# Softmax attention and soft mixture of experts: 1 / sum applied to x by GpSimd instead of to the probabilities, x transposed back for the logits, the order planned anew

## The chip, the cores and the metric

The kernel runs on one core of one Trainium2 chip. The metric is the device time of one launch in microseconds (us). The kernel before was timed three times: 593.55, 597.59 and 598.43 us, median 597.59 us.

Engine names are those of the profile: PE is TensorE (PEld its weight loads), DVE is VectorE, ACT is ScalarE, POOL is GpSimd, SP is the queue that issues the DMAs. SBUF is the on-chip memory, PSUM the accumulator memory that PE writes.

## The reference

Inputs are q, k and v of shape (8, 8, 576, 64): batch, heads, tokens, head width. All is float32.

```
scores = q @ k.T / 8                           # 576 x 576 for each head
scores = where(scores >= rowmax - tau, scores, -1e9)
attn   = exp(scores - rowmax);  attn /= (attn.sum(-1) + 1e-9)
x      = attn @ v                              # heads side by side: 4608 tokens x 512
logits = x @ phi                               # phi is 512 x 32 slots
d      = softmax of logits over the 4608 tokens
slot_input = d.T @ x                           # 32 x 512
slot_out = relu(slot_input[e] @ w1[e]) @ w2[e] # 8 experts with 4 slots each, F = 1024
c      = softmax of logits over the 32 slots
out    = c @ slot_out                          # 4608 x 512
```

Since `attn @ v` is linear in each row of attn, the division by the row's sum can be done on the probabilities, before the product with v, or on the rows of x, after it.

## The kernel before, in words

The 64 heads are worked off as 32 pairs (8 batches of 4 pairs), two heads on the two halves of the partitions. The function `pair` makes the work of one pair, `dispatch` the work that follows the fourth pair of a batch. After the last batch comes a tail with the experts and the output, which the change doesn't touch.

One pair has nine score tiles of 128 query rows by 576 keys: two heads times four row blocks of 128, and a ninth with the 64 rows left over of both heads. For each tile:

1. PE makes the scores in PSUM (L504; L509 for the ninth tile).
2. DVE finds the row's negated maximum `nmx`. Tiles 1, 3, 5 and 7 (AWAY) are moved out of PSUM by the same instruction, into the SBUF tile `ss` (L518); the others stay in PSUM (L522).
3. ACT makes exp into the SBUF tile `p` (L531; `pL` for the ninth tile).
4. POOL makes the threshold `thr` from `nmx`, one number for each row (L534).
5. DVE sets the probabilities under the threshold to 0 and sums the row into `r`, in one instruction (L538). It reads `ss` or PSUM, and `p`.
6. After two tiles of one row block, POOL adds 1e-9 to the sums (L545), DVE takes the reciprocal `ri` (L548), and POOL multiplies the probabilities of both tiles by it, 128x576 each (L552). The ninth tile has the same three steps of its own.
7. PE transposes the scaled probabilities into PSUM (L429), and ACT copies them to the SBUF tiles `pTa`, `pTb`, `pTl` (L434).

When the row blocks 0 and 1 (pTa) or 2, 3 and the left-over rows (pTb) are there, PE multiplies by v (L599, two groups of 20 matmul records). This gives x transposed, 128 (two heads of 64) x 576 tokens, which ACT copies to `xT` (L434). PE transposes the first 512 tokens of it back to token rows, and ACT copies them into the batch's tile `x`, 128 x 4 x 512. `dispatch` makes the logits from the four `xT` of the batch (L664), and later the sum `d.T @ x` from `x` (L734).

At the start of each pair POOL also multiplies the loaded keys by 1/8 (L484).

PSUM is split into four regions of two banks each. A score tile, a transposition and a pair of matmul outputs each take a region until its last reader is done. There are two `ss` tiles, four `p` tiles (each for the two heads of one row block), five `xT` and one `x`.

**What sets the order.** All of this is recorded as operations by `Order.add`, with an engine, a duration and a nominal time. `Order.plan` then goes through them with a model of the engines: an operation can start when its operands are there (LAT and SAME are the delays that it assumes after an operation) and a buffer is free; of those that can, each engine takes the one with the lowest nominal time. `TABLE` holds a correction of the nominal time for each operation: of the first, a middle and the last pair, of even, odd and last batches, and of the softmax at the end. The order that comes out is fixed: each engine works through its list strictly in that order, and an instruction that waits holds up all behind it on its engine.

## Time and profile before

| What | Value |
|---|---|
| Times of the three runs | 593.55, 597.59, 598.43 us; median 597.59 us |
| The profiled execution, first to last instruction | 595.4 us |
| Mean granted TensorE clock | 0.978 |
| Busy share of the span: PE, DVE, ACT, POOL | 92%, 83%, 75%, 69% |
| First two pairs (start of the span to the ninth tile of the second pair) | 38.0 us |
| One middle pair without dispatch | 14.67 us |
| Four middle pairs with one dispatch | 62.5 us |
| From the last pair's last copy to x to the end | 72 us |

The page gives no time of the profiled execution beside its span. The median of the three runs is 2.2 us above that span, and the span lies among the three.

A row of a group reads: line, engine, operation, output <- inputs, partitions x elements, count | busy time in us, mean ns of one | idle time of the engine just before them and what ended it. A row of the waits reads: who waited <- for whom: us in total, times, longest. A row of the chain reads: start us, duration us, what; "issue" is time in which an engine waited for nothing that the profile shows. A row of a source line reads: count: duration ns min/median/max, first and last start. A row of the stretches gives the busy us of each engine in a stretch of the span, the granted clock, the DMA share and GB/s.

### The profile page before, as it was taken

To read this page: it belongs to the slowest core of one execution; us is meant where nothing else is said; L and a number is where in the kernel's file an instruction comes from. 1 tells how busy PE (TensorE), PEld (TensorE's weight loads), DVE (VectorE), ACT (ScalarE), POOL (GpSimd) and SP (SyncE) were. 2 spreads that over 40 slices of the span, in tenths; PEclk is the share of its full clock that TensorE was granted. 3 is DMA by queue.
4 is the path that set the end of the run, shared out by engine and by line. 5 is a ranking of instruction groups with operands and counts; after the bars stand their busy time and mean duration, and the time that the engine had idled before them with its cause. 6 is when DMAs were issued, how large, how long until landed. Compare 5 with 4: busy or idle time off the path is not lost. (4 is left out here: it accounts for less than half of the span.)

```text
span 595.4 us, 17443 instructions
## 1 busy us (share of the span) xinstructions
PE 548.3 (92%) x6404; PEld 340.6 (57%) x6404; DVE 496.8 (83%) x1275; ACT 448.2 (75%) x753; POOL 410.8 (69%) x799
## 2 busy tenths in 40 slices
PE   8799999999999999999999999999999899799991
PEld 6465665555665565566666655556666465453471
DVE  5889998999999989999999999999999889231183
ACT  3588887988888888888888978898888778422071
POOL 2778886888878887888788868887888666411030
PEclk9699999999999999999999999999999989899996
DMA  6245554455445555333333333333333312799678
GB/s 167 61 94 148 160 154 137 138 147 155 129 133 158 150 154 149 83 84 84 83 85 83 85 83 83 84 83 84 84 83 84 83 32 67 245 367 407 253 306 328
DMA packets 31988, 82.97 MB, mean 139 GB/s; under 512 B 4640, under 2 KB 12832, under 8 KB 31904
## 3 DMA queue, kind: packets, MB, share of 16 engines
q1 hardware_dynamic: 31904, 81.87, 46.8%
q8 instruction: 50, 0.82, 0.6%
q14 instruction: 34, 0.28, 0.2%
HBM read 72.42 MB, written 9.44 MB: 137 GB/s over the span
## 5 line engine op out<-in xcount | busy, mean ns | idle before, releaser
L552 POOL TENSOR_SCALAR p<-p,ri 128x576 f32<-128x576 f32 x256 | 206.8, 815 | 27.2 <-DVE ri L548 11.3
L504 PE MATMUL ps<-k,q 64*128 64x288 f32 x1024 | 170.1, 437 | 16.8 <-DVE ss L518 11.3
L429 PEld LDWEIGHTS ps<-ident,p 64*128 64x128 f32 x2304 | 92.2, 140 | 59.8 <-POOL p L552 17.8
L538 DVE SCALAR_TENSOR_TENSOR p<-ss,thr,p 128x576 f32<-128x576 f32 x128 | 116.9, 915 | 4.4 <-POOL thr L534 2.9
L522 DVE TENSOR_REDUCE nmx<-ps 128x1 f32<-128x576 f32 x160 | 116.8, 752 | 4.3 <-PE ps L504 2.9
L429 PE MATMUL ps<-ident,p 64*128 64x64 f32 x2304 | 108.9, 228 | 10.0 <-POOL p L552 6.1
L504 PEld LDWEIGHTS ps<-k,q 64*128 64x128 f32 x1024 | 85.9, 190 | 51.0 <-DVE ss L518 18.7
L538 DVE SCALAR_TENSOR_TENSOR p<-ps,thr,p 128x576 f32<-128x576 f32 x128 | 101.9, 811 | 8.9 <-POOL thr L534 7.3
L531 ACT ACTIVATE p<-ss,nmx 128x576 f32<-128x576 f32 x128 | 96.7, 776 | 12.8 <-DVE ss L518 12.4
L518 DVE TENSOR_SCALAR_CACHE_REDUCE ss<-ps 128x576 f32<-128x576 f32 x128 | 96.0, 750 | 6.7 <-PE ps L504 5.4
L434 ACT COPY pTb<-ps 128x1024 f32<-128x1024 f32 (+1 forms) x95 | 82.1, 874 | 21.0 <-PE ps L429 19.2
L531 ACT ACTIVATE p<-ps,nmx 128x576 f32<-128x576 f32 x128 | 91.9, 739 | 6.4 <-DVE nmx L522 3.9
L534 POOL TENSOR_SCALAR thr<-nmx,nabs 128x1 f32<-128x1 f32 x160 | 70.6, 445 | 11.2 <-DVE nmx L522 6.3
L599 PE MATMUL ps<-pTb,vv 128*64 128x320 f32 x512 | 76.0, 439 | 1.9 <-ACT pTb L434 1.7
L434 ACT COPY pTa<-ps 128x1024 f32<-128x1024 f32 x64 | 64.8, 1012 | 11.5 <-PE ps L429 8.6
L545 POOL TENSOR_SCALAR ri<-r 128x2 f32<-128x2 f32 (+1 forms) x160 | 38.9, 243 | 48.4 <-DVE p L538 21.0
L599 PE MATMUL ps<-pTa,vv 128*64 128x256 f32 x512 | 65.5, 400 | 0.0
L599 PEld LDWEIGHTS ps<-pTb,vv 128*64 128x64 f32 x512 | 33.9, 136 | 30.7 <-ACT pTl L434 2.2
L534 POOL TENSOR_SCALAR thr<-nmx,pabs 128x1 f32<-128x1 f32 x128 | 36.6, 286 | 15.8 <-DVE ss L518 10.9
L599 PEld LDWEIGHTS ps<-pTa,vv 128*64 128x64 f32 x512 | 35.2, 142 | 18.1 <-issue 2.2
L599 PE MATMUL ps<-pTl,vv 128*64 128x256 f32 (+1 forms) x256 | 41.9, 406 | 0.0
L859 POOL TENSOR_TENSOR c<-lall,crow 128x512 f32<-128x512 f32 x9 | 9.3, 1043 | 43.9 <-PE ct L421 38.9
(133 smaller groups left out, 605.4 us busy)
## 6 DMA issues: line engine op xcount, KB each, us to landing
w<-in_w SPq DMA_DIRECT2D x44, 512.0 KB, 6.7
q<-in_qT SPq DMA_DIRECT2D x62, 288.0 KB, 4.6
vv<-in_vt SPq DMA_DIRECT2D x32, 320.0 KB, 3.1
host<-in_w SPq DMA_DIRECT2D x20, 512.0 KB, 6.1
k<-in_kT SPq DMA_DIRECT2D x62, 144.0 KB, 4.9
out<-w SPq DMA_DIRECT2D x8, 512.0 KB, 3.3
out<-host SPq DMA_DIRECT2D x8, 512.0 KB, 5.0
out<-host SPq DMA_DIRECT2D x4, 256.0 KB, 4.4
```

Of the source, the lines that this page charges most:

```text
L429: nc.tensor.transpose(out=s[:, g, c:c + 64], in_=ins[g], identity=ident[rows[g], rows[g]], tile_position=(64 * g, 0))
L434: G.add("ACT", 51 + 0.833 * n, nom, lambda: nc.scalar.copy(*io()), r, w)
L504: nc.tensor.matmul(s.t[:, g, 0:HS], qt.t[rows[g], h, c * 128:(c + 1) * 128], kt.t[rows[g], h * HS:(h + 1) * HS], start=True, stop=True, ti ...
L518: dve(729, t + OFF['mx'], [s], [ss, nmx], lambda s=s, ss=ss, nmx=nmx: nc.vector.tensor_scalar(out=ss.t.rearrange("p (a k) -> p a k", a=2), ...
L522: dve(665, t + OFF['mx'], [s], [nmx], lambda s=s, nmx=nmx: nc.vector.tensor_reduce(out=nmx.t, in_=s.t[:, :, 0:HS], axis=AX.XY, op=ALU.max, ...
L531: G.add("ACT", 624, t + OFF['ex'], lambda sv=sv, nmx=nmx, view=view, away=away: nc.scalar.activation(view().rearrange("p (a k) -> p a k", ...
L534: pool(250, t + OFF['th'], lambda nmx=nmx, thr=thr, away=away: nc.gpsimd.tensor_scalar(out=thr.t, in0=nmx.t, scalar1=1.0 if away else -1.0 ...
L538: lambda sv=sv, thr=thr, view=view, i=i, away=away: nc.vector.scalar_tensor_tensor(out=view().rearrange("p (a k) -> p a k", a=2), in0=sv() ...
L545: pool(200, t + OFF['ri'], lambda e=e: nc.gpsimd.tensor_scalar(out=ri.t[:, e], in0=r.t[:, e], scalar1=1e-9, scalar2=1.0, op0=ALU.add, op1= ...
L552: pool(725, t + OFF['sc'], lambda k=k, view=view_: nc.gpsimd.tensor_scalar(out=view(), in0=view(), scalar1=ri.t[:, k:k + 1], **one), [ri[c ...
L599: nc.tensor.matmul(lone(w)[h * 64:(h + 1) * 64, 0:n], vv.t[:, v0:v0 + 64], p0, start=(kb == 0), stop=(kb == 4), tile_position=(0, h * 64), ...
L859: nc.gpsimd.tensor_tensor(out=c4, in0=lall[:, rows].unsqueeze(2).to_broadcast([128, k, 4, NS]), in1=crow[:, rows].unsqueeze(2).unsqueeze(3 ...
```

## The change

- **Probabilities stay unscaled.** In the pairs 0 to 30 the eight multiplications of `p` (L552) fall away. Of the five additions of 1e-9 and five reciprocals of a pair two each are left: one for the eight tiles of the row blocks, on 128x8, and one for the ninth tile. The ninth tile is still scaled as before, and the last pair (`late`) keeps all of the old way.
- **x is scaled token by token.** The product with v and the copies to `xT` and `x` work as before on unscaled numbers. Then POOL multiplies the pair's 128 columns of `x` by `ri`, one number for each token and head (128 x 4 x 128, one instruction).
- **x is transposed back.** The logits are made from `xT`, so PE transposes the scaled columns of `x` (eight transpositions of 64 columns) into a PSUM region, and ACT copies this over the first 512 tokens of `xT`. The 64 tokens left over are right already.
- **The order is planned anew.** The planner's delays are now given by pairs of engines (CROSS), some durations change, an operation may take longer until its result counts as there (`more`), and one that reads `ss` is given more time while POOL is busy (`port`). All numbers of TABLE are new, with a row for the three new operations.

The diff, cut to its core:

```
-LAT = {"PE": 197, "DVE": 140, "ACT": 152, "POOL": 160, "SP": 4500}
+LAT = {"PE": 252, "DVE": 150, "ACT": 165, "POOL": 86, "SP": 4500}
+CROSS = {("PE", "DVE"): 260, ("DVE", "ACT"): 182, ("DVE", "POOL"): 220, ("ACT", "DVE"): 237, ("ACT", "POOL"): 250,
+         ("POOL", "DVE"): 61, ("POOL", "ACT"): 100}
...
     ("pair", [
-        -3.06, -29.12, -61.01, -39.19, 30.02, -2.11, -10.54, -76.24, -2.37, 48.53, -1.04, -55.17, 28.40, 59.52,
+        -3.30, 5.50, 61.88, -311.91, 3.65, -52.04, -125.74, 257.90, -294.44, -98.37, -52.64, 88.74, 299.51, -268.05,
...
+    ("new", [
+        682.26, -933.80, 448.94,
+    ]),
...
+                if o[7]:
+                    end += 0.4 * max(0.0, min(engfree["POOL"] - t, o[1]))
+                    held = end
+                if eng == "POOL" and held > t:
+                    end += held - t
                 if eng == "PE":
-                    end += SWITCH * (o[5] != mode)
+                    end += SWITCH * (o[5] != mode) + 50 * (engfree[eng] < t)
...
-                    lat = (SAME if ops[j][0] == eng else LAT)[eng]
+                    lat = SAME[eng] if ops[j][0] == eng else CROSS.get((eng, ops[j][0]), LAT[eng]) + o[6]
...
+        late = p == NP - 1
...
-            if h == 1 or i == 8:
+            if i == 8 or late and h == 1:
                 e = slice(i // 2 * 2, i + 1)
-                pool(200, t + OFF['ri'], lambda e=e: nc.gpsimd.tensor_scalar(
+                pool(292, t + OFF['ri'], lambda e=e: nc.gpsimd.tensor_scalar(
                     out=ri.t[:, e], in0=r.t[:, e], scalar1=1e-9, scalar2=1.0, op0=ALU.add, op1=ALU.mult),
                     [r[k] for k in range(e.start, e.stop)], [ri[c]])
...
+            elif not late and h == 1:
+                if i == 7:
+                    pool(292, t + OFF['ri'], lambda: nc.gpsimd.tensor_scalar(
+                        out=ri.t[:, 0:8], in0=r.t[:, 0:8], scalar1=1e-9, scalar2=1.0, op0=ALU.add, op1=ALU.mult),
+                        [r[k] for k in range(8)], [ri[0]])
+                    dve(84, t + OFF['ri'], [], [ri[0]], lambda: nc.vector.reciprocal(ri.t[:, 0:8], ri.t[:, 0:8]))
+                    G.skip(2)
+                else:
+                    G.skip(4)
...
+        if not late:
+            xj = lambda: x.t[:, :, j * 128:(j + 1) * 128]
+            wide = lambda: xj().rearrange("p c (h d) -> p c h d", h=2)
+            G.add("POOL", 1040, u + 6.8, own="new", r=[ri[0]], w=[x[j]], fn=lambda: nc.gpsimd.tensor_tensor(
+                out=wide(), in0=wide(), in1=ri.t[:, 0:8].rearrange("p (c h) -> p c h", h=2).unsqueeze(3).to_broadcast(
+                    [128, 4, 2, 64]), op=ALU.mult))
+            w = Buf("s")
+            G.add("PE", 248, u + 7, own="new", r=[x[j]], w=[w], fn=lambda w=w: [
+                nc.tensor.transpose(out=w.t[:, g, c * 64:c * 64 + 64], in_=xj()[rows[g], c],
+                                    identity=ident[rows[g], rows[g]], tile_position=(64 * g, 0))
+                for c in range(4) for g in range(2)])
+            G.add("ACT", 477, u + 7.3, own="new", r=[w], w=[xT[0], xT[1]], fn=lambda w=w: nc.scalar.copy(
+                xT.t[:, 0:SM].rearrange("p (c g q) -> p g c q", c=4, g=2),
+                w.t[:, :, 0:256].rearrange("p g (c q) -> p g c q", c=4)))
```

The lines of the new kernel are 16 to 40 higher: L521 and L526 are the scores, L535 and L539 the maxima, L551 the threshold, L555 the cut, L562 and L573 the addition of 1e-9, L569 the scaling of the ninth tile, L501 that of the keys, L640 the new multiplication, L645 the new transposition, L445 the other transpositions, L625 the product with v.

POOL's list in a middle pair of the kernel before (p20 to p23 are the four row blocks, pL0 the ninth tile, thr thresholds, ri and r reciprocals and sums, k1 the next keys):

```order
L545 TENSOR_SCALAR ri0_157<-r0_154 128x2
L552 TENSOR_SCALAR p23_180<-p23_180,ri0_157 128x576 x2
L545 TENSOR_SCALAR ri0_157<-r0_154 128x2
L534 TENSOR_SCALAR thr2_166<-nmx0_160,nabs_98 128x1
L534 TENSOR_SCALAR thr0_164<-nmx3_163,nabs_98 128x1
L534 TENSOR_SCALAR thr3_167<-nmx2_162,pabs_100 128x1
L545 TENSOR_SCALAR ri0_157<-r0_154 128x1
L552 TENSOR_SCALAR pL0_168<-pL0_168,ri0_157 128x576
L552 TENSOR_SCALAR p22_179<-p22_179,ri0_157 128x576 x2
L534 TENSOR_SCALAR thr1_165<-nmx1_161,pabs_100 128x1
L534 TENSOR_SCALAR thr2_166<-nmx0_160,nabs_98 128x1
L484 TENSOR_SCALAR k1_184<-k1_184,flag8_90 128x576
```

Thresholds stand here behind and between the multiplications of 128x576. The same engine in a middle pair of the new kernel, from the last threshold of a pair to the first four of the next and on (x0 is the batch's x; ri1 belongs to the pair before the one of ri2):

```order
L551 TENSOR_SCALAR thr3_167<-nmx2_162,nabs_98 128x1
L562 TENSOR_SCALAR ri2_159<-r2_156 128x1
L640 TENSOR_TENSOR x0_141<-x0_141,ri1_158 128x4x128
L569 TENSOR_SCALAR pL0_168<-pL0_168,ri2_159 128x576
L501 TENSOR_SCALAR k1_184<-k1_184,flag8_90 128x576
L551 TENSOR_SCALAR thr0_164<-nmx3_163,pabs_100 128x1
L551 TENSOR_SCALAR thr3_167<-nmx1_161,nabs_98 128x1
L551 TENSOR_SCALAR thr2_166<-nmx2_162,nabs_98 128x1
L551 TENSOR_SCALAR thr1_165<-nmx0_160,pabs_100 128x1
L573 TENSOR_SCALAR ri2_159<-r2_156 128x8
```

The three large multiplications of a pair now stand in one block, with x first, and the next pair's thresholds stand behind it.

DVE's list in the new kernel around the same place, from the cuts of a pair's last tiles to the first cuts of the next (p is the row block, r2 the old pair's sums, r0 the new one's):

```order
L555 SCALAR_TENSOR_TENSOR pL0_168,r2_156<-ps0_223,thr2_166,pL0_168 128x576
L555 SCALAR_TENSOR_TENSOR p23_180,r2_156<-ss1_173,thr0_164,p23_180 128x576
L555 SCALAR_TENSOR_TENSOR p21_178,r2_156<-ss0_172,thr3_167,p21_178 128x576
L535 TENSOR_SCALAR ss1_173,nmx3_163<-ps2_225 128x576
L565 RECIPROCAL ri2_159<-ri2_159 128x1
L535 TENSOR_SCALAR ss0_172,nmx0_160<-ps2_225 128x576
L539 TENSOR_REDUCE nmx1_161<-ps0_223 128x1
L539 TENSOR_REDUCE nmx2_162<-ps3_226 128x1
L555 SCALAR_TENSOR_TENSOR p20_177,r0_154<-ss1_173,thr1_165,p20_177 128x576
L555 SCALAR_TENSOR_TENSOR p22_179,r0_154<-ps0_223,thr2_166,p22_179 128x576
```

The kernel before has maxima and cuts mixed at this place:

```order
L538 SCALAR_TENSOR_TENSOR pL0_168,r0_154<-ps0_223,thr1_165,pL0_168 128x576
L548 RECIPROCAL ri0_157<-ri0_157 128x2
L538 SCALAR_TENSOR_TENSOR p21_178,r1_155<-ps3_226,thr2_166,p21_178 128x576
L548 RECIPROCAL ri0_157<-ri0_157 128x1
L518 TENSOR_SCALAR ss1_173,nmx1_161<-ps2_225 128x576
L522 TENSOR_REDUCE nmx0_160<-ps0_223 128x1
L538 SCALAR_TENSOR_TENSOR p21_178,r1_155<-ss0_172,thr0_164,p21_178 128x576
L538 SCALAR_TENSOR_TENSOR p20_177,r1_155<-ss1_173,thr1_165,p20_177 128x576
L538 SCALAR_TENSOR_TENSOR p20_177,r1_155<-ps0_223,thr3_167,p20_177 128x576
```

In the new list the maxima of four or five tiles stand together, and then their cuts.

PE's list in a middle pair of the kernel before, from the transposition of xT on (ps0 to ps3 are the PSUM regions):

```order
L429 MATMUL ps2_225<-ident_61,xT4_140 128x64 x8
L504 MATMUL ps3_226<-k0_189,q0_190 128x288 x2
L504 MATMUL ps1_224<-k0_189,q0_190 128x288 x2
L429 MATMUL ps2_225<-ident_61,p20_177 128x64 x16
L504 MATMUL ps1_224<-k0_189,q0_190 128x288 x2
L504 MATMUL ps0_223<-k0_189,q0_190 128x288 x2
L429 MATMUL ps2_225<-ident_61,p23_180 128x64 x16
L599 MATMUL ps3_226<-pTa0_169,vv1_153 64x256 x8
```

And of the new kernel:

```order
L445 MATMUL ps1_224<-ident_61,xT4_140 128x64 x8
L445 MATMUL ps3_226<-ident_61,p20_177 128x64 x16
L521 MATMUL ps0_223<-k0_189,q0_190 128x288 x2
L445 MATMUL ps1_224<-ident_61,p23_180 128x64 x16
L521 MATMUL ps3_226<-k0_189,q0_190 128x288 x2
L521 MATMUL ps2_225<-k0_189,q0_190 128x288 x2
L645 MATMUL ps1_224<-ident_61,x0_141 128x64 x8
L625 MATMUL ps0_223<-pTa0_169,vv1_153 64x256 x8
```

The new transposition of x takes a region of its own between the scores and the product with v.

37 lines of the change are left out of this document (21 added, 16 removed), and 46 rows, old and new, of the table TABLE.

## The prediction

> **What bounds the kernel now.** First the page, then the busy time by stretches: one middle pair (14.67 us, from one turn of the chain below to the next) and four middle pairs with one dispatch. The columns are the stretch and its length, busy us of PE, PEld, DVE, ACT, POOL, then clock, DMA share, GB/s.
>
> ```profile
> span 595.4 us, 17443 instructions
> PE 548.3 (92%) x6404; PEld 340.6 (57%) x6404; DVE 496.8 (83%) x1275; ACT 448.2 (75%) x753; POOL 410.8 (69%) x799
> ```
>
> ```profile
> 428.89:443.56 14.67, 13.86 (x172) 8.96 (x170) 14.12 (x37) 12.89 (x22) 12.41 (x25) 1.00 0.35 82
> 414.22:428.89 14.67, 13.91 (x173) 8.84 (x172) 13.44 (x36) 12.61 (x22) 12.03 (x25) 1.00 0.30 74
> 82.39:144.91 62.52, 59.30 (x737) 36.59 (x735) 58.11 (x151) 53.05 (x88) 50.29 (x98) 1.00 0.52 147
> ```
>
> In the pairs all four engines are at 82% and above, DVE and PE at about 95%. The clock is full and the DMA engines are half idle. So no engine alone is the bound; the pair repeats as a loop through all of them. The chain of waits over one turn shows which work is in the loop (start, duration, what).
>
> ```profile
> 428.89 1.29 POOL p L552 x2
> 430.18 0.15 issue
> 430.33 0.52 POOL pL L552
> 430.85 0.21 issue
> 431.06 0.76 POOL thr L534
> ...
> 434.76 0.76 POOL p L552
> 435.52 0.08 issue
> 435.60 0.71 PE ps L429 x16
> 436.31 2.84 PE ps L599 x20
> 439.15 0.65 PE ps L509 x8
> ```
>
> Twice in a turn POOL holds the others up: a threshold on which DVE waits stands behind three multiplications (428.89 to 431.82, 2.9 us), and a transposition waits for a multiplication (434.76 to 435.60, 0.8 us). Summed over the run, the waits say the same (waiter, released by: us, times, longest).
>
> ```profile
> PEld ps L429 <- POOL p L552: 17.8, 26, 1.4
> DVE p L538 <- POOL thr L534: 10.2, 55, 0.4
> DVE ri L548 <- POOL ri L545: 8.9, 22, 2.0
> PEld ps L504 <- DVE ss L518: 18.7, 31, 1.7
> ```
>
> **The change part by part.** The groups that it touches (busy, mean ns | idle before):
>
> ```profile
> L552 POOL TENSOR_SCALAR p<-p,ri 128x576 f32<-128x576 f32 x256 | 206.8, 815 | 27.2 <-DVE ri L548 11.3
> L484 POOL TENSOR_SCALAR k<-k,flag 128x576 f32<-128x576 f32 x31 | 26.5, 855 | 6.0 <-DMA k<-in_kT 3.8 <-PE ps L429 0.6
> L552 POOL TENSOR_SCALAR pL<-pL,ri 128x576 f32<-128x576 f32 x32 | 24.0, 749 | 1.8 <-DVE ri L548 1.7
> L545 POOL TENSOR_SCALAR ri<-r 128x2 f32<-128x2 f32 (+1 forms) x160 | 38.9, 243 | 48.4 <-DVE p L538 21.0
> L548 DVE RECIPROCAL ri<-ri 128x2 f32<-128x2 f32 x128 | 20.4, 159 | 8.8 <-POOL ri L545 8.2
> L859 POOL TENSOR_TENSOR c<-lall,crow 128x512 f32<-128x512 f32 x9 | 9.3, 1043 | 43.9 <-PE ct L421 38.9
> L434 ACT COPY x<-ps 128x512 f32<-128x512 f32 x32 | 18.8, 589 | 5.9 <-PE ps L429 5.9
> L538 DVE SCALAR_TENSOR_TENSOR p<-ss,thr,p 128x576 f32<-128x576 f32 x128 | 116.9, 915 | 4.4 <-POOL thr L534 2.9
> L522 DVE TENSOR_REDUCE nmx<-ps 128x1 f32<-128x576 f32 x160 | 116.8, 752 | 4.3 <-PE ps L504 2.9
> ```
>
> *POOL* loses in each of 31 pairs 8 x 0.815 + 3 x 0.243 = 7.2 us and gains one multiplication of 128x512 with two inputs, 1.04 us by L859. Of its 12.2 us in a turn about 6 are left: it is no bound any more.
>
> [...]
>
> *DVE* loses three reciprocals. One takes 0.16 us, but the rows below show the next cut starting 0.08 us after it, so 3 x 0.08 = 0.24 us. And cuts that read `ss` get shorter where POOL is idle (count: ns min/median/max; a threshold for later):
>
> ```profile
> 439.45 0.16 DVE L548 RECIPROCAL ri<-ri 128x2 f32<-128x2 f32 x1
> 439.53 0.80 DVE L538 SCALAR_TENSOR_TENSOR p<-ss,thr,p 128x576 f32<-128x576 f32 x1
> ```
>
> ```profile
> L538 DVE SCALAR_TENSOR_TENSOR p<-ss,thr,p x128: 790/820/1334, 9.0 to 505.5; 128x576 f32<-128x576 f32 x128
> L538 DVE SCALAR_TENSOR_TENSOR p<-ps,thr,p x128: 796/814/820, 12.1 to 509.2; 128x576 f32<-128x576 f32 x128
> L534 POOL TENSOR_SCALAR thr<-nmx,nabs x160: 258/267/855, 10.8 to 508.9; 128x1 f32<-128x1 f32 x160
> ```
>
> Cuts with both inputs in SBUF have a long tail; cuts from PSUM never pass 820 ns. The mean of 915 lies 125 ns over the minimum: 4 x 0.125 = 0.5 us a pair, of which a third may stay, since about a third of POOL's long work stays (1.04 + 0.75 + 0.86 of 8.1 us). I take a gain of 0.4. DVE's mean of the two turns, (14.12 + 13.44) / 2 = 13.78, falls to 13.78 - 0.24 - 0.40 = 13.14 us.
>
> *DVE's idle time* is now 14.67 - 13.78 = 0.89 us a pair. Of the waits for POOL (10.2 + 8.9 us, less 2.0 at the start) 17.1 / 31 = 0.55 is a pair's share. If all go, 0.34 is left; if others take their place, 0.89. I take 0.7, near the upper end, because the thresholds of the new list still stand behind a block of POOL (below) and PE gets fuller. The pair then takes 13.14 + 0.7 = 13.85 us; the ends are 13.5 and 14.0.
>
> *PE* gains eight transpositions of 64 columns and perhaps a change of mode. Steps from start to start, and the first product with v from the chain:
>
> ```profile
> 439.90 0.41 PE L429 MATMUL ps<-ident,xT 64*128 64x64 f32 x8
> 440.15 1.19 PE L504 MATMUL ps<-k,q 64*128 64x288 f32 x8
> 441.18 0.66 PE L429 MATMUL ps<-ident,p 64*128 64x64 f32 x16
> ```
>
> ```profile
> 415.35 2.31 PE ps L599 x20
> ```
>
> Eight transpositions take 0.25 us, two score tiles 1.03. At best a pair is 8 tiles (4.12), the ninth (0.65), 90 transpositions at 0.031 (2.8), and the products 2.84 + 2.31: 12.7 us, after the change 13.0. The other end is PE's present busy time, whose ends are modelled: 13.9 + 0.25 = 14.15. DVE's 13.85 lies between, so PE can follow, but with little to spare.
>
> *ACT* gains a copy of 0.59 us: (12.89 + 12.61) / 2 + 0.59 = 13.3 of 13.85. It fits, but tightly, and the copy stands where only the logits wait for it.
>
> *The path to the logits* becomes longer by about 1.04 + 0.25 + 0.59 us and the hand-overs, once a batch. Dispatch has the whole next pair as its cover, and the fifth `xT` holds it; without that cover it would cost 2 us x 7 = 14. The last pair keeps the old path, so nothing is added ahead of the tail.
>
> *Start:* DVE waits 2.0 us for POOL's first reciprocal (the longest wait in the row above); this goes. Tail: unchanged, and moved as a whole.
>
> **The sum.** (14.67 - 13.85) x 31 pairs = 25.4, with pairs beside a dispatch taken alike, + 2.0 at the start: 27.4 us. 595.4 - 27.4 = 568.0; the median stood 2.2 over the span: **570 us**.
>
> **The rivals.**
> 1. *PE or ACT takes over.* With the chain's step of 0.71 us for 16 transpositions PE needs 4.12 + 0.65 + 90 x 0.044 + 5.15 + 0.25 = 14.1 us, and both engines get work while DVE loses it. With half of DVE's idle time as waits (0.35) the pair takes 14.45: 0.22 x 31 + 2 = 9 us gained, 589 us. For it: both are near 95% of 13.85.
> 2. *PSUM regions bind.* PE waits 18.7 us for DVE to empty a region. The new transposition holds one for 0.25 + 0.59 and hand-overs, about 1.05 of 4 x 14.67 us: 1.8%. If this is the bound, the pair takes 14.67 to 14.93 us, the kernel 596 to 604. Against it: POOL, not regions, was in the loop above.
> 3. *A collision a pair.* x's multiplication holds up a cut from `ss` for its whole 1.04 us: DVE 14.18, the pair 14.88, 595.4 + 0.21 x 31 - 2 + 2.2 = 602 us. The traced worst hold-up is 1334 - 790 = 544 ns, less than one multiplication (749); with it the pair takes 14.4 and the kernel 587. Against both: in the new order x's turn comes when DVE passes to maxima from PSUM. [...]
> 4. *Slower: thresholds behind the block.* In the new list x (1.04), the ninth tile (0.75) and the keys (0.86) stand ahead of the next pair's first threshold. DVE covers them with two maxima into `ss` and two plain ones, 3 us at most. If x starts late because ACT copies `x` late, or the keys land late, DVE stands, with four cuts queued behind the first, and PE behind these. If x and the ninth tile fall out of the cover, that is 1.79 x 31 = 55 - 27 = 28 us more: 626 us. It decides from 27.4 / 31 = 0.9 us a pair. For it: the keys' row has 3.8 us of waits for the DMA. Against it: only the ninth tile and the keys hang on DVE's second place in the block, and 0.75 + 0.86 + 0.27 = 1.9 us fit into three maxima of 0.75.
>
> **How the numbers follow.** Forecast (553 to 580): 0.62. Rival 1 (580 to 591): 0.15. Rivals 2 and 3 within 1%: 0.08 and 0.03. Rival 4: 0.12. One per cent, about what a measurement can tell from no change, is 591.6 to 603.6. So faster 0.77, same 0.11, slower 0.12. The low end is PE at its best, 13.0, with 0.3 of waits: 1.37 x 31 + 2 = 44.5, 553 us. Up to 595 the range takes in rival 1 and a part of 2 and 3; beyond lie 0.12 + 0.04, below it 0.04.
>
> **What would show it.** Right: a middle pair of 13.5 to 14.0 us; POOL at about half of its busy time in the pairs; the mean of cuts from `ss` at 0.80 to 0.85 us; waits of PE for POOL's `p` gone, and in their place waits for DVE's cuts. Rival 1: PE over 96% in a pair, DVE idle and waiting for scores. Rival 2: waits of the scores for DVE and ACT grown. Rival 3: cuts over 1.2 us in every pair. Rival 4: DVE's waits for thr L551 over 0.5 us each. Wrong altogether: a pair of 14.6 us or more.

## The result, and the profile after

The kernel after takes **571.94 us** (median; 571.28 to 572.87) against 596.94 us (593.55 to 598.43, now four runs) of the kernel before: a ratio of 0.960 with a 95% interval of 0.957 to 0.964. The forecast was 570.0 us. One run further down, of new_double_mult, took 736.9 us at a mean granted clock of 0.65 against 0.98 to 0.99 in its nine others and is left out of its numbers.

The page, and then busy time by stretches: one middle pair (two turns of it stand here, since the prediction showed two), one pair with dispatch, and the 24 pairs from the ninth tile of the sixth pair to that of the thirtieth. The columns are as before: stretch, length, busy us of PE, PEld, DVE, ACT, POOL, then clock, DMA share, GB/s.

```profile
span 570.3 us, 17258 instructions
PE 542.1 (95%) x6652; PEld 341.2 (60%) x6652; DVE 475.0 (83%) x1182; ACT 451.8 (79%) x784; POOL 223.8 (39%) x489
```

```profile
403.08:417.01 13.93, 13.85 (x180) 8.88 (x178) 13.29 (x34) 12.57 (x23) 6.33 (x14) 1.00 0.36 89
417.01:430.99 13.98, 13.89 (x179) 8.88 (x179) 13.25 (x34) 12.91 (x23) 6.50 (x14) 1.00 0.36 90
430.99:447.44 16.45, 16.26 (x216) 10.28 (x216) 14.61 (x39) 15.21 (x28) 6.80 (x16) 1.00 0.29 75
88.06:447.44 359.38, 353.94 (x4634) 226.27 (x4632) 332.71 (x838) 322.44 (x562) 157.12 (x343) 1.00 0.40 109
```

The same 24 pairs of the kernel before:

```profile
98.76:470.35 371.59, 355.00 (x4442) 222.49 (x4440) 349.20 (x909) 319.64 (x538) 300.77 (x582) 1.00 0.41 106
```

POOL's busy time is halved (300.77 to 157.12 us), DVE's is 16.5 us shorter, PE's hardly changes, and the stretch is 12.2 us shorter. PE is now busy for 98.5% of it (353.94 / 359.38), before 95.5%.

The chain of waits over a good half of a middle pair of the kernel after (start, duration, what); up to 417.01 us, where the next turn starts, it goes on with PE alone:

```profile
403.15 0.64 PE ps L526 x8
403.80 2.84 PE ps L625 x20
406.64 0.69 PE ps L521 x4
407.33 0.13 PE ps L445 x4
407.46 0.02 issue
407.48 0.28 ACT pTl L450
407.76 0.58 ACT x L450
408.34 0.93 ACT pTa L450
409.27 0.04 issue
409.31 1.24 PE ps L521 x8
410.55 0.34 PE ps L645 x8
```

POOL, which held the others up twice in a turn, is out of the chain, and so is DVE. What is left is PE with one excursion over three copies of ACT, 1.79 us. The waits of the whole run and the groups and source rows (count: ns min/median/max) that answer to those shown of before:

```profile
PEld ps L445 <- DVE p L555: 9.5, 24, 0.8
DVE p L555 <- POOL thr L551: 2.0, 7, 0.6
DVE ri L565 <- POOL ri L562: 1.7, 2, 1.2
```

```profile
L555 DVE SCALAR_TENSOR_TENSOR p<-ss,thr,p 128x576 f32<-128x576 f32 x128 | 103.6, 822 | 0.3 <-ACT p L548 0.3
L640 POOL TENSOR_TENSOR x<-x,ri 128x512 f32<-128x512 f32 x31 | 37.4, 1206 | 7.6 <-ACT x L450 7.0
L648 ACT COPY xT<-ps 128x512 f32<-128x512 f32 x31 | 18.3, 590 | 0.2
```

```profile
L555 DVE SCALAR_TENSOR_TENSOR p<-ss,thr,p x128: 711/814/1507, 9.7 to 484.0; 128x576 f32<-128x576 f32 x128
L640 POOL TENSOR_TENSOR x<-x,ri x31: 1042/1152/1512, 33.6 to 489.6; 128x512 f32<-128x512 f32 x31
```

DVE's waits for thresholds fell from 10.2 to 2.0 us, those for reciprocals from 8.9 to 1.7, and the mean cut from `ss` from 915 to 822 ns. The waits of PE's weight loads for POOL's scaled p (17.8 us) are gone; waits for DVE's cuts (9.5 us) stand at this place now, but 7.3 us of them were there before.

### The profile page after: what moved, and what is told of

It reads as the page before. It is cut to its first block, busy times and chain, and to the rows that moved or that the text cites. A ratio compares the mean times of both kernels' runs of the same rounds, so it can differ in the third digit from the quotient of the medians.

```text
span 570.3 us, 17258 instructions
## 1 busy us (share of the span) xinstructions
PE 542.1 (95%) x6652; PEld 341.2 (60%) x6652; DVE 475.0 (83%) x1182; ACT 451.8 (79%) x784; POOL 223.8 (39%) x489
## 4 chain that ended last, share of the span: by engine, by line
PE 76%; ACT 11%; DVE 6%; issue 3%; POOL 1%; DVEq 0%; POOLq 0%; ACTq 0%
PE ps L625 27%; PE ps L521 20%; PE ps L445 11%; ACT pTa L450 4%; PE ps L526 3%; PE h L934 3%; PE so L968 2%; ACT x L450 2%; PE ps L645 2%; PE ps L774 2%; DVE p L555 2%; PE ps L704 1%; PE ps L437 1%; ACT pTl L450 1%; ACT p L548 1%
## 5 line engine op out<-in xcount | busy, mean ns | idle before, releaser
L521 PE MATMUL ps<-k,q 64*128 64x288 f32 x1024 | 166.1, 430 | 3.7 <-ACT pTb L450 0.9
L539 DVE TENSOR_REDUCE nmx<-ps 128x1 f32<-128x576 f32 x160 | 113.2, 750 | 1.1 <-PE ps L521 0.2
L535 DVE TENSOR_SCALAR_CACHE_REDUCE ss<-ps 128x576 f32<-128x576 f32 x128 | 96.1, 753 | 13.7 <-ACT pTb L450 5.3
L555 DVE SCALAR_TENSOR_TENSOR p<-ps,thr,p 128x576 f32<-128x576 f32 x128 | 102.0, 814 | 4.9 <-ACT p L548 2.7
L521 PEld LDWEIGHTS ps<-k,q 64*128 64x128 f32 x1024 | 85.0, 187 | 33.3 <-issue 6.9
L445 PEld LDWEIGHTS ps<-ident,p 64*128 64x128 f32 x2304 | 91.1, 138 | 22.4 <-DVE p L555 6.6
L445 PE MATMUL ps<-ident,p 64*128 64x64 f32 x2304 | 103.3, 224 | 1.1 <-DVE p L555 0.4
L555 DVE SCALAR_TENSOR_TENSOR p<-ss,thr,p 128x576 f32<-128x576 f32 x128 | 103.6, 822 | 0.3 <-ACT p L548 0.3
L548 ACT ACTIVATE p<-ss,nmx 128x576 f32<-128x576 f32 x128 | 94.8, 780 | 10.2 <-DVE ss L535 10.2
L551 POOL TENSOR_SCALAR thr<-nmx,nabs 128x1 f32<-128x1 f32 x160 | 53.7, 338 | 72.7 <-DVE p L555 36.5
L551 POOL TENSOR_SCALAR thr<-nmx,pabs 128x1 f32<-128x1 f32 x128 | 38.0, 297 | 111.1 <-DVE ss L535 109.3
L625 PE MATMUL ps<-pTb,vv 128*64 128x320 f32 x512 | 76.0, 439 | 0.4 <-ACT pTb L450 0.4
L625 PE MATMUL ps<-pTa,vv 128*64 128x256 f32 x512 | 63.9, 393 | 1.4 <-ACT pTa L450 1.4
L625 PEld LDWEIGHTS ps<-pTb,vv 128*64 128x64 f32 x512 | 33.9, 136 | 38.1 <-DVE nmx L539 9.6
L450 ACT COPY xT<-ps 128x256 f32<-128x256 f32 (+1 forms) x63 | 25.5, 405 | 28.6 <-PE ps L625 16.5
L625 PEld LDWEIGHTS ps<-pTa,vv 128*64 128x64 f32 x512 | 34.5, 139 | 20.8 <-issue 3.9
L625 PE MATMUL ps<-pTl,vv 128*64 128x256 f32 (+1 forms) x256 | 41.9, 406 | 0.0
L640 POOL TENSOR_TENSOR x<-x,ri 128x512 f32<-128x512 f32 x31 | 37.4, 1206 | 7.6 <-ACT x L450 7.0
L562 POOL TENSOR_SCALAR ri<-r 128x1 f32<-128x1 f32 (+1 forms) x36 | 21.0, 584 | 37.3 <-DVE pL L555 36.6
```

Source lines behind the costliest of these rows:

```text
L445: nc.tensor.transpose(out=s[:, g, c:c + 64], in_=ins[g], identity=ident[rows[g], rows[g]], tile_position=(64 * g, 0))
L450: G.add("ACT", 51 + 0.833 * n, nom, lambda: nc.scalar.copy(*io()), r, w)
L521: nc.tensor.matmul(s.t[:, g, 0:HS], qt.t[rows[g], h, c * 128:(c + 1) * 128], kt.t[rows[g], h * HS:(h + 1) * HS], start=True, stop=True, ti ...
L535: dve(674, t + OFF['mx'], [s], [ss, nmx], lambda s=s, ss=ss, nmx=nmx: nc.vector.tensor_scalar(out=ss.t.rearrange("p (a k) -> p a k", a=2), ...
L539: dve(665, t + OFF['mx'], [s], [nmx], lambda s=s, nmx=nmx: nc.vector.tensor_reduce(out=nmx.t, in_=s.t[:, :, 0:HS], axis=AX.XY, op=ALU.max, ...
L548: G.add("ACT", 668 if away else 630, t + OFF['ex'], lambda sv=sv, nmx=nmx, view=view, away=away: nc.scalar.activation(view().rearrange("p ...
```

## The experiments

The change has two sides: other operations, and another order of all operations. The theory of the prediction was that POOL's load sets the pair, so that taking the scaling off POOL brings the gain. The rival is that the order brings it. The table shows all kernels by three stages, cut at the starts of the ninth tiles of the sixth and the thirtieth pair (read off PE's timeline), from one profiled execution each. Kernels with the same middle pairs agree there within 0.3 us (before and old_fill 371.6 and 371.4, after and new_last_too both 359.4). Where the ninth tile stands within the work of its pair depends on the order, so across orders start and end compare only roughly; the 24 pairs are whole rounds of the loop in each. The ratio, with its 95% interval, compares the runs with runs of the kernel before taken beside them (medians 595.2 to 597.3 us), so it is not the quotient of two medians of the table.

| Kernel | Start to 6th pair | 24 pairs | 30th pair to end | Median us | Ratio to before |
|---|---|---|---|---|---|
| before | 98.8 | 371.6 | 125.1 | 596.94 | 1 |
| after | 88.1 | 359.4 | 122.9 | 571.94 | 0.960 [0.957, 0.964] |
| old_small_scale | 98.4 | 367.8 | 122.7 | 588.56 | 0.986 [0.984, 0.988] |
| new_ops_old_order | 93.5 | 384.6 | 127.5 | 608.16 | 1.020 [1.018, 1.022] |
| old_replanned | 93.9 | 358.7 | 128.1 | 582.47 | 0.977 [0.974, 0.980] |
| old_replanned_small | 95.4 | 356.1 | 127.8 | 578.94 | 0.971 [0.968, 0.973] |
| old_replanned_more | 91.1 | 361.5 | 126.8 | 581.8 | 0.977 [0.974, 0.980] |
| new_small_mult | 87.6 | 359.4 | 121.0 | 570.88 | 0.957 [0.955, 0.959] |
| new_double_mult | 90.2 | 373.7 | 127.2 | 590.03 | 0.992 [0.989, 0.995] |
| new_small_back | 87.3 | 356.7 | 122.8 | 569.42 | 0.956 [0.952, 0.960] |
| new_last_too | 87.9 | 359.4 | 127.9 | 576.36 | 0.968 [0.964, 0.971] |
| old_fill | 97.2 | 371.4 | 124.9 | 595.09 | 0.997 [0.995, 0.999] |
| old_more_pe | 100.4 | 377.3 | 124.9 | 602.69 | 1.009 [1.006, 1.011] |
| new_more_pe | 88.3 | 362.0 | 121.8 | 574.66 | 0.962 [0.961, 0.964] |

### POOL's scaling made small in the old order

```
-                    pool(725, t + OFF['sc'], lambda k=k, view=view_: nc.gpsimd.tensor_scalar(
-                        out=view(), in0=view(), scalar1=ri.t[:, k:k + 1], **one), [ri[c]], [dst_])
+                    cut = slice(0, S if i == 8 or p == NP - 1 else 1)
+                    pool(725, t + OFF['sc'], lambda k=k, view=view_, cut=cut: nc.gpsimd.tensor_scalar(
+                        out=view()[:, cut], in0=view()[:, cut], scalar1=ri.t[:, k:k + 1], **one), [ri[c]], [dst_])
```

> The kernel before in its old order, but POOL's multiplication of the eight row-block tiles of a pair (L552) is made on 1 of 576 columns (pairs 0 to 30), so most probabilities stay unscaled and the output is not the reference's. Every instruction, wait and place in the lists stays. Theory A (POOL's long work in the loop and against DVE's cuts is what cost the time): a middle pair of 13.7 to 14.2 us instead of 14.67, cuts from ss at about 0.80 us instead of 0.915, 570 to 580 us. Theory B (the new order brings the gain): cuts get shorter, but the pair stays over 14.4 us, 588 to 597 us.

```profile
98.35:466.12 367.77, 352.46 (x4443) 222.93 (x4441) 341.32 (x909) 317.95 (x538) 204.63 (x582) 1.00 0.41 107
```

POOL is a third less busy in the 24 pairs (300.77 to 204.63 us) and DVE 7.9 us less, but the stretch is only 3.8 us shorter, the whole kernel 1.4%. In the old order, making POOL's scaling small brings about a third of the gain (the eight instructions are still there; by the drop of 96.1 us over 192 of them, whose mean was 815 ns before, some 0.3 us each is left, an estimate). What held the pair up in its place was not traced.

### The new operations in the old order

```
-LAT = {"PE": 252, "DVE": 150, "ACT": 165, "POOL": 86, "SP": 4500}
-CROSS = {("PE", "DVE"): 260, ("DVE", "ACT"): 182, ("DVE", "POOL"): 220, ("ACT", "DVE"): 237, ("ACT", "POOL"): 250,
-         ("POOL", "DVE"): 61, ("POOL", "ACT"): 100}
+LAT = {"PE": 197, "DVE": 140, "ACT": 152, "POOL": 160, "SP": 4500}
+CROSS = {}
...
-    ("new", [
-        682.26, -933.80, 448.94,
-    ]),
```

Against the kernel after, this takes the planner's new delays away (`more`, `port` and the 50 ns too) and has the TABLE of the kernel before, without numbers for the new operations. The operations and their durations are the new ones.

> The new kernel's operations, with the old planner's delays and the old TABLE; the three new operations stand at their nominal times without a correction. Theory A: within 1.5% of the new kernel, 570 to 580 us. Theory B: the gain is mostly gone, 588 us or more.

```profile
93.45:478.09 384.64, 360.35 (x4634) 224.33 (x4632) 337.04 (x837) 326.88 (x561) 151.59 (x342) 1.00 0.39 102
```

POOL has 151.59 us to do here, DVE as little as in the kernel after, and yet the stretch is 13 us *longer* than before. So the operations without an order made for them lose 2%. Less work on POOL and DVE is by itself no gain in this order.

### The old operations in an order of their own

```
-        late = p == NP - 1
+        late = True
```

The old operations with the new kernel's own TABLE (old_ops_new_order, the numbers that it lacks set to -300) have no time: the planner found no order for them. So an order of their own was sought. This is the kernel after with the old way in all pairs, the planner's new delays kept, and new numbers in TABLE that were sought for these operations.

> The operations of the kernel before, unchanged (probabilities scaled by POOL, no transposition back), but planned with the new planner's delays and with a TABLE of its own that was sought for these operations; as in the new order, the maxima of four or five tiles now mostly stand together, and then their cuts. Theory B1 (a better order alone brings the gain): 576 us or less. Theory C (the order brings a part, and the work taken off POOL the rest): 580 to 592 us. Theory A (POOL's work alone): 594 us or more.

```profile
93.87:452.52 358.65, 351.19 (x4440) 219.16 (x4440) 339.96 (x910) 318.03 (x537) 299.00 (x583) 1.00 0.41 110
437.92:452.52 14.60, 14.25 (x180) 9.06 (x178) 13.55 (x37) 13.55 (x23) 12.36 (x25) 1.00 0.36 85
```

The 24 pairs take 358.65 us with all of POOL's scaling (299.00 us busy), as little as those of the kernel after (359.38). This speaks against the prediction's reason: in the middle, an order alone brings the whole gain, without taking any work off POOL. In the median it brings 14.4 of 25.0 us.

What the new operations are worth pair by pair can't be read off the two kernels. Of four pairs of the kernel before and of the kernel after, two are free of a dispatch's work; over the 24 pairs these took 14.80 us on average before and 13.98 after, the others 16.16 and 15.97. In old_replanned the dispatch is spread over all four pairs (the row of 14.60 us holds 180 matmul records of PE, a pair before without dispatch 172), so its pairs can't be set beside these one by one.

The same order with the scaling cut to one column tells what POOL's scaling is worth there:

```
-                        out=view(), in0=view(), scalar1=ri.t[:, k:k + 1], **one), [ri[c]], [dst_])
+                        out=view()[:, cut], in0=view()[:, cut], scalar1=ri.t[:, k:k + 1], **one), [ri[c]], [dst_])
```

> The same order as in the run before this, with POOL's eight multiplications of a pair made on 1 of 576 columns (pairs 0 to 30; the output is not the reference's). Theory C: 8 us or more under the run before this, 568 to 580 us, since in this order POOL's work is what is left in the way. Theory B1: within 3 us of it.

It is 2.6 us in the 24 pairs and 3.5 us in the median: again little, in a second order.

At the end the old operations in their new order were still some 10 us slower than the kernel after, by start and end (93.9 and 128.1 us against 88.1 and 122.9). The numbers of TABLE were sought on, with rows for the first and last pair:

```
-        -254.13, -262.93, -121.49, -359.87, -442.00, -323.11, -95.98, -37.27, -173.13, -143.71, 117.34, 141.76, -249.83, -376.39,
...
+        -285.65, -271.11, 244.36, 225.18, -503.69, -536.81, -309.20, 26.62, 216.24, -290.96, -217.33, -475.32, 93.46, -310.31,
```

> The operations of the kernel before once more in an order of their own, by the delays of the new planner; the numbers of TABLE were sought on, with rows of their own for the first and the last pair, since the middle pairs of the first such order already ran as fast as those of the kernel after (358.7 against 359.4 us for 24 pairs) and only start and end were slower (93.9 against 88.1 us, 128.1 against 122.9 us). Theory: the order brings the middle pairs, but start and end need the new operations too (without them POOL's scaling stands in front of the transpositions when nothing else is there to hide it): 577 to 581 us, no faster than 575. Rival: the order alone can bring it all, the first search was only too short: 570 to 574 us.

It came out at 581.8 us, just above the range of its theory: the start 2.8 us shorter, the end 1.3, the 24 pairs 2.9 longer, the ratio the same. TensorE's clock is a part of the difference in the start: it was halved for 6.8 us there in old_replanned, for 3.4 in old_replanned_more and not at all in the kernel after. The order alone did not reach the kernel after in two searches; that no order could is not shown.

### What the added work costs in the kernel after

Four edits of the kernel after price its three new operations and the exception for the last pair. In the first the multiplication of x is made on 128x8 of its 128x512 numbers:

```
-                out=wide(), in0=wide(), in1=ri.t[:, 0:8].rearrange("p (c h) -> p c h", h=2).unsqueeze(3).to_broadcast(
-                    [128, 4, 2, 64]), op=ALU.mult))
+                out=wide()[:, :, :, 0:1], in0=wide()[:, :, :, 0:1], in1=ri.t[:, 0:8].rearrange("p (c h) -> p c h", h=2).unsqueeze(3),
+                op=ALU.mult))
```

> The new kernel, but POOL's multiplication of x is made on 1 of 64 columns of each head and token row (128x8 instead of 128x512), so x is mostly unscaled and the output is not the reference's. If POOL is off the path after the change, as forecast: 570 to 573 us. If the multiplication still holds up cuts (mean 0.822, longest 1.507 us) or the transposition behind it, 0.1 to 0.3 us a pair come back: 562 to 569 us.

In the 24 pairs it changes nothing (359.38 and 359.38 us), in the median 1.1 us. POOL's multiplication is hidden there. How much more could be hidden is told by making it twice:

```
-            G.add("POOL", 1040, u + 6.8, own="new", r=[ri[0]], w=[x[j]], fn=lambda: nc.gpsimd.tensor_tensor(
+            G.add("POOL", 1040, u + 6.8, own="new", r=[ri[0]], w=[x[j]], fn=lambda: [nc.gpsimd.tensor_tensor(
...
-                    [128, 4, 2, 64]), op=ALU.mult))
+                    [128, 4, 2, 64]), op=ALU.mult) for _ in range(2)])
```

> The new kernel, but POOL's multiplication of x by 1 / sum is made twice in a row (so x is divided by the sum twice and the output is not the reference's); 1.04 to 1.2 us of POOL more in each pair, ahead of the next pair's thresholds and of the transposition back. This is the place of the forecast's fourth rival. In the new trace a first threshold ends about 0.3 us before DVE can use it. If that is all the cover: 0.6 to 0.9 us a pair, 590 to 600 us. If POOL's place has room for it: 571 to 576 us.

The waits of that run (waiter, released by: us, times, longest), and one middle pair:

```profile
PE ps L645 <- POOL x L640: 9.3, 25, 1.5
PE ps L445 <- DVE p L555: 8.0, 21, 0.8
DVE p L555 <- POOL thr L551: 20.9, 27, 1.2
```

```profile
417.75:432.38 14.63, 14.12 (x180) 9.02 (x178) 13.02 (x34) 13.06 (x23) 7.37 (x15) 1.00 0.34 85
```

One more multiplication, 1.04 us, costs 0.7 us in a pair without dispatch (13.93 to 14.63), 0.6 on average over the 24, and 18 us in the median. POOL is busy for only half of the pair, and yet the added time is paid, since POOL stands at one place in two paths: DVE's first cut waits for a threshold behind the block, and PE's transposition back waits for x, with the product with v queued behind it. Of the 1.04 us some 0.3 to 0.4 were cover. This is rival 4 of the prediction in the flesh: the threshold behind the block (waits of 20.9 us instead of 2.0), and beside it the wait for x. By this one point it begins with some 0.4 us of delay.

The transposition back, cut from eight to two (the copy from 512 to 128 columns):

```
-                for c in range(4) for g in range(2)])
+                for c in range(1) for g in range(2)])
...
-                xT.t[:, 0:SM].rearrange("p (c g q) -> p g c q", c=4, g=2),
-                w.t[:, :, 0:256].rearrange("p g (c q) -> p g c q", c=4)))
+                xT.t[:, 0:128].rearrange("p (c g q) -> p g c q", c=1, g=2),
+                w.t[:, :, 0:64].rearrange("p g (c q) -> p g c q", c=1)))
```

> The new kernel, but PE transposes back 2 of the 8 blocks of x and ACT copies 128 of 512 columns to xT, so three quarters of the tokens have logits from unscaled x and the output is not the reference's. PE does 0.19 us less in a pair, ACT 0.32 us. If PE is the bound after the change: 0.19 x 31 = 6 us less, 565 us, and down to 557 us if ACT's copy is in the way too. If the added work is hidden: 570 to 573 us.

It gives 2.6 us in the 24 pairs, 0.11 us a pair, for six transpositions of PE (0.19 us by the prediction's step) and most of a copy of ACT. Even with all of it put down to PE, little more than half of PE's added time is paid; the run does not part PE from ACT.

The new way for the last pair too:

```
-        late = p == NP - 1
+        late = False
```

> The new kernel, with the new way for the last pair also. After the last cut the old way needs a reciprocal and two multiplications of 0.75 us before the last transpositions, the new way 1.04 us of POOL, 0.25 of PE and 0.59 of ACT with their hand-overs before the logits. If only the length of that path counts: 572 to 574 us. If POOL's eight multiplications hold up the last pair: 568 to 571 us.

It came out at 576.36 us, above both ranges. All of it is in the end (122.9 to 127.9 us), and the exception is worth 4.4 us of the median. How much of this is the longer path to the logits is open: 1.5 us of it stand ahead of the last pair's ninth tile already, the last pair's numbers in TABLE were sought for the old way, and between that tile and the last 13 us TensorE's clock was halved for 10.2 us here, for 3.4 in the kernel after.

### Is PE the bound now?

With PE at 98.5% a new theory was at hand: PE has become the bound, as rival 1 has it. Eight transpositions made twice, in both kernels at the same place, test it:

```
-                    for h in range(2) for k in range(4)])
+                    for h, k in [(0, k) for k in range(4) if c == 0] + [(h, k) for h in range(2) for k in range(4)]])
```

> The kernel before; of the 16 transpositions of the first row block eight are made twice in each of the 32 pairs, over the same place: some 0.25 to 0.35 us more of PE a pair, nothing else changed, the order the same. Theory: PE is not what sets the pair of the kernel before (95.5% busy in the 24 middle pairs, with waits for POOL in its loop), so that at most half of it is seen: under 5 us. Rival: PE with its queue sets the pair already here: 0.3 x 32 = 8 to 11 us.

> The kernel after, with the same addition: eight transpositions of the first row block made twice in each pair, 0.25 to 0.35 us of PE. Theory: PE (98.5% busy in the 24 middle pairs) now sets the pair, and each us more of it is a us more of the kernel: 8 to 11 us, 580 to 583 us. Rival: the pair is still set by a loop through all engines, with DVE at 92.6%, and PE's share hides: under 5 us, 573 to 577 us.

The 24 pairs of the kernel before with the addition, and of the kernel after with it:

```profile
100.35:477.65 377.30, 360.48 (x4634) 228.84 (x4633) 349.53 (x909) 319.01 (x538) 302.32 (x582) 1.00 0.40 104
```

```profile
88.32:450.36 362.04, 357.43 (x4827) 233.13 (x4825) 332.35 (x838) 322.67 (x562) 157.02 (x343) 1.00 0.40 109
```

It came out the other way round. In the 24 pairs the kernel before pays 5.7 us for the added work (371.59 to 377.30), 0.24 us a pair, all of the prediction's 0.25 for eight transpositions; its median of 602.69 us lies between the two expectations. The kernel after pays 2.7 us (359.38 to 362.04), 0.11 us a pair. So the theory fell: PE's share of busy time, whose ends are modelled, does not tell that PE is the bound, and at 95.5% of the kernel before its transpositions stood in the loop, while at 98.5% more than half of an added one is hidden. PE's timeline shows where it is hidden. In a pair without dispatch of the kernel after, and then of the same kernel with the addition (start, duration, what):

```profile
414.71 0.71 PE L445 MATMUL ps<-ident,p 64*128 64x64 f32 x16
415.26 1.75 PE L521 MATMUL ps<-k,q 64*128 64x288 f32 x12
417.01 0.72 PE L526 MATMUL ps<-k,q 64*64 64x288 f32 x8
```

```profile
417.40 0.96 PE L445 MATMUL ps<-ident,p 64*128 64x64 f32 x24
418.20 1.68 PE L521 MATMUL ps<-k,q 64*128 64x288 f32 x12
419.81 0.71 PE L526 MATMUL ps<-k,q 64*64 64x288 f32 x8
```

From start to start the transpositions take 0.25 us longer (0.55 to 0.80), and the scores behind them 0.14 less (1.75 to 1.61). So PE stood there for 0.14 us that its busy time doesn't show, and the rest is paid: PE is near its bound in this pair, with a small wait hidden in its busy time. With new_small_back, where 0.11 us a pair came out too, this fits a pair of several paths of nearly the same length, PE's among them; the chain above shows only the one that ended last.

### The start, and TensorE's clock

The start is 10.7 us shorter, and the prediction had 2.0 us there besides the pairs. The stretches of the start of the kernel before:

```profile
15.00:20.00 5.00, 1.95 (x28) 1.13 (x23) 4.42 (x12) 2.71 (x4) 3.94 (x10) 0.92 0.29 72
20.00:25.00 5.00, 4.37 (x32) 3.13 (x34) 4.78 (x13) 2.97 (x6) 3.50 (x9) 0.50 0.53 108
25.00:30.00 5.00, 5.00 (x26) 2.43 (x24) 3.42 (x9) 2.12 (x3) 4.17 (x8) 0.56 0.00 2
```

PE has 1.95 us to do in 5, and then the granted clock is 0.50 for 10.2 us, from 19.2 us on. In the kernel after it is 1.00 all through the start. Does the clock follow the idle time, and what does it cost? In the kernel before, PE was given work that nobody needs ahead of it:

```
-                for g in range(2):
+                for g in [*range(2)] * (3 if (p, i) == (0, 8) else 2 if (p, i) == (0, 6) else 1):
```

> The kernel before, its order untouched; in the first pair alone PE makes the scores of the ninth tile three times (14.5 us of its span) and those of one other tile behind it twice, each time over the same PSUM region. This fills PE where it had 1.95 of 5.00 us busy (15 to 20 us) with some 1.8 us of work. Theory: the stretch of half TensorE clock (10.2 us from 19.2 us on in the kernel before) follows PE's idle time ahead of it, and costs up to half its length, 5.1 us. Then it is gone or shorter, the sixth pair's ninth tile starts at 94 to 97 us instead of 98.8, and the time is 592 to 595 us. Rival: the clock goes down for another reason, or nothing waits for PE there: the stretch stays, and the added work costs 0 to 1.8 us: 597 to 599 us.

```profile
15.00:20.00 5.00, 3.79 (x52) 2.27 (x44) 4.71 (x12) 2.99 (x5) 3.96 (x9) 1.00 0.20 53
20.00:25.00 5.00, 4.03 (x43) 2.32 (x42) 4.92 (x14) 3.30 (x6) 3.69 (x9) 1.00 0.58 124
25.00:30.00 5.00, 4.66 (x72) 3.17 (x70) 4.56 (x12) 3.70 (x5) 4.74 (x9) 1.00 0.00 2
```

The clock stays at 1.00, and the kernel is *faster* with the useless work, by a little less than expected: the second pair's ninth tile starts at 35.2 instead of 38.0 us, though only 1.5 us are left of this at the sixth pair, and 0.3% (0.1 to 0.5) of the time. So in these two runs the clock followed PE's idle time (0.50 behind 1.95 us busy of 5.00, 1.00 with 3.79), and the stretch at half clock cost 2.8 us at the place, net of the added work. Of the 9.2 us that the kernel after has gained at the third pair's ninth tile (52.9 to 43.7 us) this is a third. The order of the first pairs can bring most of the rest: with the old operations old_replanned gains 4.9 us and old_replanned_more 7.7 us at the sixth pair, although their clock is halved for a while.

## Why the prediction was right or wrong

**The number** was right: 570.0 us forecast, 571.94 measured. Two of its terms were wrong in size, in opposite directions (7.5 us too much in the 24 pairs, 4.6 too little in the start), so that the sum comes out so close is luck; and the reason that it gave for the main term holds only in part.

- **The middle pair**, 13.85 us (13.5 to 14.0) forecast, 13.93 and 13.98 measured. Its parts hold as well: DVE was to lose 0.64 us a pair and lost 16.5 / 24 = 0.69; the cuts from `ss` were to have a mean of 0.80 to 0.85 us and have 0.822; DVE's idle time was to be 0.7 us and is 13.93 - 13.29 = 0.64 and 13.98 - 13.25 = 0.73. POOL, forecast at about 6 us, has 6.33 and 6.50. The gain comes out as well: the twelve pairs without dispatch among the 24 took 14.80 us on average before (14.65 to 15.08; the 14.67 of the prediction is one of the short ones) and take 13.98 after, 0.82 us less.
- **"With pairs beside a dispatch taken alike"** is the step that failed. The pairs without dispatch gained 0.82 us, those with a part of one 0.19 (16.16 to 15.97 on average); over all, a pair gained 12.2 / 24 = 0.51 us instead of 0.82. For the 24 pairs the sum had 19.7 us.
- **The start** was mis-sized the other way: up to the sixth pair the sum had 2.0 + 5 x 0.82 = 6.1 us, and 10.7 came. DVE's wait of 2.0 us for POOL was rightly seen, and it went, but neither its reason nor what it set off was. POOL was not busy then: it stood for 2.25 us waiting for the DMA of the next keys, and the first addition of 1e-9 stood behind these in its list.

```profile
14.53 0.74 POOL L484 TENSOR_SCALAR k<-k,flag 128x576 f32<-128x576 f32 x1 [2.25 <-DMA k<-in_kT]
15.36 0.19 POOL L545 TENSOR_SCALAR ri<-r 128x2 f32<-128x2 f32 x1
15.58 0.17 DVE L548 RECIPROCAL ri<-ri 128x2 f32<-128x2 f32 x1 [2.02 <-POOL ri L545]
```

  PE then stood for the DVE instruction behind the reciprocal (1.21 us, the first row of the last section), and TensorE went to half clock (2.8 us by old_fill). The end gave 2.2 us against 1.6; besides the last 12 us, TensorE's clock was halved there for 6.8 us before and 3.4 after, so this need not come from the pairs.
- **What the gain rests on.** The prediction read the chain of waits as POOL holding the others up twice in a turn, and took the gain from POOL's load. With POOL's scaling nearly taken away in the old order, 3.8 of 12.2 us came in the 24 pairs (old_small_scale); with all of it kept in a new order, 12.9 us (old_replanned); with the new operations and the old order, 13 us were lost (new_ops_old_order). So in the 24 pairs it is the order; the new operations gain only together with an order made for them, and the some 10 us that the old operations in the best order found still lack stand in start and end. What in the order brings it was not isolated.
- **PE**: 0.25 us more a pair was forecast; the transpositions back and their copies are half hidden (new_small_back). PE's busy time of 13.85 us lies between the ends 13.0 and 14.15.
- **ACT**: 13.3 us forecast, 12.57 and 12.91 measured. The step counted the copy at its full 0.59 us. Added up one by one over the 24 pairs, ACT's instructions grew from 348.7 to 366.0 us, but its busy time, in which overlaps count once, only from 319.6 to 322.4. So in the trace of after they overlap by 43.6 us on 562 instructions, 0.08 us each. The prediction had taken such an overlap into account for DVE's reciprocals (0.16 us long, the next cut 0.08 us behind the start) and not for ACT.
- **The path to the logits** was said to be hidden. In the last pair the new way costs 4.4 us (new_last_too), in part perhaps by this path, and the kernel avoids it; with a dispatch the pairs gained least, and whether the longer path is the reason is open: shortening its multiplication (new_small_mult) brought nothing in the 24 pairs.
- **Rival 1** (PE takes over) had as its sign PE over 96% in a pair. The sign came (99.4%: 13.85 / 13.93), the rival didn't: the pair is at the forecast, and more than half of an added piece of PE's work is hidden. The sign was badly chosen. **Rival 2** (PSUM regions): of the scores' waits for `ss` (18.7 us) 6.6 are left; over all, the waits of the scores' weight loads for DVE fell from 35 to 16 us and those for ACT rose from 13.5 to 16.7. No run tested regions by themselves. **Rival 3** (a collision a pair): only 2 of the 128 cuts from `ss` took over 0.9 us (1337 and 1507 ns), where 54 did before; in old_replanned, with all of POOL's scaling and the same operations on DVE, DVE is busy for 9.2 us less in the 24 pairs than before (349.20 to 339.96 us), so this too goes by the order. The prediction set the worst hold-up, 544 ns, against a whole multiplication of 749. But in the kernel before all 69 cuts from `ss` that began in a POOL instruction with over 0.2 us of it left ended 601 to 611 ns after its end, however early in it they had begun: a cut that began in the middle was held up only for what was left (rows in the last section). **Rival 4** (thresholds behind the block): not reached, 2.0 us of waits in all, but nearer than the prediction thought: it saw 0.9 us of gain to be eaten first, and by new_double_mult the loss begins after 0.3 to 0.4 us.

POOL's multiplication of x, 128x512 with two inputs, takes 1.21 us on average (L640) and costs nothing in the 24 pairs (new_small_mult); no run had DVE do it. That POOL is idle for half of the time is not enough for this, as new_double_mult shows: what counts is the cover at its place in the list.

## What to carry to other kernels

In a kernel whose engines are all above 80% and whose order is fixed, a change of operations and the order made for it can't be priced apart: run the new operations in the old order and the old operations in a new one, and only then say what brought the gain. A chain of waits shows the path that ended last, not how far behind it the next one is; an addition of a few tenths of a us at one place, in both kernels, tells this better than the share of busy time. A sum that comes out right may hold two errors that cancel, so compare it stage by stage, here start, pairs without dispatch, pairs with one, and end, and see to it that the stages compared hold the same work.

## What was not expected of the hardware

- TensorE's granted clock fell to 0.50 for 10.2 us behind a stretch in which PE was busy for 1.95 of 5.00 us, and stayed at 1.00 with 3.79 of 5.00 (old_fill). The stretch at half clock in the start was of 6.8 us in old_replanned and of 3.4 in new_ops_old_order and old_replanned_more, and there was none in the kernel after. The shortest stretches at half clock in the kernel before, from 476.54 and from 510.67 us on, took 3.41 us. In a stretch of that length ahead of the fall PE was busy for 1.47 us in the kernel before, 1.74 in old_replanned and 1.62 in new_ops_old_order, 43 to 51% of it; where no fall came, the emptiest such stretches of the start had 2.2 us (the kernel after, from 18.15 us on) and 2.1 us (old_fill, from 17.05). PE's longest single gaps in the kernel before were 1.21 us and, begun 0.5 us ahead of the fall at 19.15 us, 1.10 us:

```profile
16.46 0.76 PE L504 MATMUL ps<-k,q 64*128 64x288 f32 x4 [1.21 <-DVE ss L518]
17.96 0.71 PE L429 MATMUL ps<-ident,p 64*128 64x64 f32 x16 [0.74 <-POOL thr L534]
19.77 2.36 PE L504 MATMUL ps<-k,q 64*128 64x288 f32 x8 [1.10 <-ACT pTa L434]
```

- POOL's instructions and DVE's cuts from `ss`, which have both inputs in SBUF, held each other up. In the kernel before, cuts from `ss` took 790 to 819 ns where they did not begin in a POOL instruction, and up to 1334 ns where they did; cuts from PSUM took 796 to 820 ns, also the 76 that began in a POOL instruction with over 0.2 us of it left. A cut that takes about 0.81 us alone, in the kernel before and then in the kernel after:

```profile
158.11 0.74 POOL L552 TENSOR_SCALAR p<-p,ri 128x576 f32<-128x576 f32 x1
158.13 1.33 DVE L538 SCALAR_TENSOR_TENSOR p<-ss,thr,p 128x576 f32<-128x576 f32 x1
```

```profile
469.80 1.04 POOL L640 TENSOR_TENSOR x<-x,ri 128x512 f32<-128x512 f32 x1 [0.66 <-ACT x L450]
469.95 1.51 DVE L555 SCALAR_TENSOR_TENSOR p<-ss,thr,p 128x576 f32<-128x576 f32 x1
```

  Both cuts end about 0.61 us after POOL's instruction. It holds the other way round too, and gives the spread of POOL's multiplication of 128x512 by two inputs, 1042 to 1512 ns with a mean of 1206: the 8 that met no cut from `ss` took 1042 to 1045 ns, and the 21 that began during one ended 899 to 904 ns after it. In the new order it is mostly POOL that stands and not DVE: 21 of the 31 multiplications of x, against 2 of the 128 cuts from `ss` over 0.9 us.
